# Linear attention and a two-layer feed-forward block in one kernel: a ring of 1280 tokens, accumulators in other banks for late blocks, and plain fp32 projections in the first two batches

## The chip, the cores and the metric

The kernel runs on one core of one Trainium2 chip. The metric is the device time of one execution in microseconds; the kernel before has a median of 1211.63 us over three runs (1211.42 to 1212.69). A profile is one more execution, with its own time. Five engines work side by side, each through its own queue in a fixed order: TensorE (PE in the profile, its weight loads PEld), VectorE (DVE), ScalarE (ACT), GpSimd (POOL) and SyncE (SP), which issues all DMAs here.

## The reference

Eight batches of 576 tokens with 8 heads of 64 features; tokens are then rows of 512 features.

```
def phi(x):
    proj = einsum('bhsd,df->bhsf', x, w_phi)
    proj = proj - max(abs(proj), axis=-1, keepdims=True)
    return concatenate([exp(proj), exp(-proj)], axis=-1)
q_p, k_p = phi(q), phi(k)
kv = einsum('bhsf,bhsd->bhfd', k_p, v)
z = sum(k_p, axis=2)
num = einsum('bhsf,bhfd->bhsd', q_p, kv)
den = einsum('bhsf,bhf->bhs', q_p, z)[..., None] + 1e-06
x = (num / den) with heads joined to rows of 512, 4608 rows
h = x @ w_in                # 512 x 2048
out = maximum(0.01 * h, h) @ w_out      # 2048 x 512
```

The weights w_in and w_out come as 64-bit floats and are taken apart on the chip.

## The kernel before

**Number formats.** Most products are made of three single-pass matmuls in fp32r: an operand is split into a high half (a cast) and a low half (the difference), and high x high, high x low and low x high are added in PSUM. Where both operands of a matmul are plain fp32 tiles, one matmul does it; the trace shows such a matmul as two records.

**Attention.** Two heads form a head pair, number i = 4 b + hp for batch b. `k_phase(i)` loads keys and values, projects 576 tokens in five pieces (`proj`, lines 302 to 306), takes the largest absolute value (VectorE), subtracts it, takes two exponentials (ScalarE) and sums key features times values into kv. `token_q_phase` or `q_phase` does the same for the queries and multiplies by kv; the result is divided by the denominator (line 433 and its like, on GpSimd) and stands in `ring`. Batches 0 and 1 (i under 8) work with plain fp32 kv products, but their projections are three fp32r matmuls per piece: `rk` and `rq` are split before (lines 196, 197, 351, 352, 452, 453, 522 to 524), and the block-diagonal w_phi is held in two halves `bd_h` and `bd_l`. Batch 0 has functions of its own (`first_k_phase`, `first_q_phase`), which borrow the room of weight group 3 (tag "late": `fr1`, `f2`, `f3`, `fr4`) and of the ring. Keys and values 2 and 3 land in the places of 0 and 1 once those are split.

**Weights.** `load_weights` takes 32 pieces of 512 KB: a DMA into one of two stages (one of them in the ring, heads 2 and 3 of batch 1), then three ScalarE and five VectorE instructions that make an fp32 number of the two words of a 64-bit float (lines 159 to 165) and split it into halves (167, 168).

**Feed-forward.** 18 blocks of 256 tokens. `split(i)` (604) splits the block's x from the ring into `xh`, `xl`. `layer1(i, ft)` makes 12 matmuls of 256 columns for each of 16 column groups ft, then a leaky ReLU and a split (625 to 627). `layer2` (630) follows three steps later with 6 matmuls of 512 columns into two PSUM banks of tag "acc", which are emptied to `o` and sent out at the last ft (643 to 646).

**Order.** The loop at 678 interleaves the steps; `advance` draws attention's generators along, up to `room(i)` batches. A scheduler then arranges every engine's instructions by priority (`tc.cur_priority`, lower first): batch 0's keys and first queries, its other queries (`PU`), the rest of attention (`PA`), the weights (`PW`), the feed-forward steps (0). The ring has room for two batches; a batch's places are free once all blocks that read the batch two before are split. PSUM has eight banks: 3 of tag "a", 1 "c", 2 "h", 2 "acc".

Of the kernel before, what the change touches and what calls it, by code (L numbers as in the profile page):

```python
# [44 lines left out]
def attention_moe_kernel(ctx: ExitStack, tc: tile.TileContext, q, k, v, vt, w_phi, w_in, w_out, out):  # L45
# [43 lines left out]
    ring = ct([P, 2, NP, S], F32, "ring")  # L89
# [4 lines left out]
    bd = st([P, 2, 2 * F], F32R, "bd")  # L94
    bd_h, bd_l = bd[:, 0], bd[:, 1]
# [5 lines left out]
    fr1, fr4 = (cp.tile([P, 2048], F32R, tag="late", name=n, bufs=4) for n in ("fr1", "fr4"))  # L101
    f2, f3 = (cp.tile([P, 2048], F32, tag="late", name=n, bufs=4) for n in ("f2", "f3"))
# [8 lines left out]
    def first_load_k(i):  # L111
        if i % 2 == 0:
            rk = st([P, S], F32, "rk")
            rv = st([P, 10, 66], F32, "rv")
        else:
            rk = part(f2, 0, [S])
            rv = part(f2, S, [10, 66])
        nc.sync.dma_start(rk, k[i])
        first_k[i] = rk, rv

    def first_load_v(i):
        rv = first_k[i][1]
# [16 lines left out]
    nc.gpsimd.memset(bd_h.bitcast(F32), 0.0)  # L139
    nc.gpsimd.memset(bd_l.bitcast(F32), 0.0)  # L140
    for j in range(2):
        r = slice(64 * j, 64 * j + 64)
        c = slice(F * j, F * j + F)
        nc.scalar.copy(bd_h[r, c], wr[r])
        nc.vector.tensor_tensor(bd_l[r, c], wr[r], wq_h[r].bitcast(F32), op=ALU.subtract)

    def load_weights():
        n = 0
        stages = [x.rearrange(pat)[:, 0:1024].bitcast(I32) for x, pat in (
            (ring[:, 1, 2:4], "p a s -> p (a s)"), (st([P, 2, 2, U], F32, "qh"), "p a b s -> p (a b s)"))]  # L150
        for ft in range(NFT):
            for which, src in ((0, w_in), (1, w_out)):
                raw = stages[n % 2]
                nc.sync.dma_start(raw, src[:, ft].bitcast(I32))
# [4 lines left out]
                nc.scalar.activation(w, top.bitcast(F32), AF.Abs)
                nc.vector.tensor_scalar(w, w, TINY, HUGE, op0=ALU.max, op1=ALU.min)  # L160
# [4 lines left out]
                nc.vector.tensor_tensor(wi, wi, cr, op=ALU.add)  # L165
# [24 lines left out]
    def k_phase(i):  # L190
        nat = i < NK
        rk, rv = kraw.pop(i)
        ks = st([P, 2, S], F32R, "ks")
        kh, kl = ks[:, 0], ks[:, 1]
        if nat:
            copy_("kh", kh, rk)
            tt_("kl", kl, rk, kh.bitcast(F32), ALU.subtract)
        else:
# [9 lines left out]
        yield  # L208
# [93 lines left out]
    def proj(pk, s, lh, ll, n=P):  # L302
        o = pk[0:n, 256 * s : 256 * s + 256]
        nc.tensor.matmul(o, lhsT=lh, rhs=bd_h, start=True, stop=False)
        nc.tensor.matmul(o, lhsT=lh, rhs=bd_l, start=False, stop=False)
        nc.tensor.matmul(o, lhsT=ll, rhs=bd_h, start=False, stop=True)

    def q_group(qh, ql, t0, w, kvh, x, pm, dn):
# [37 lines left out]
    def token_q_phase(i):  # L346
        b, hp = divmod(i, NP)
        rq = qraw.pop(i)
        qs = st([P, 2, S], F32R, "qs")
        qh, ql = qs[:, 0], qs[:, 1]  # L350
        copy_("qx", qh, rq)
        tt_("qr", ql, rq, qh.bitcast(F32), ALU.subtract)
        if i + 1 < B * NP:
            load_q(i + 1)
        yield
        tq = st([P, 2, 2, U], F32, "tq").rearrange("p a b c -> p a (b c)")
        for g, (t0, w) in enumerate(units):
            yield from q_group(qh, ql, t0, w, kvs_of[i][0], ring[:, b % 2, hp, t0 : t0 + w],
                               tq[:, g % 2, 0:DM].rearrange("p (a f) -> p a f", f=F), st([P, U], F32, "dn")[:, 0:w])

    def q_phase(i):
# [36 lines left out]
        for j in range(2):  # L398
# [16 lines left out]
            for u in range(2):  # L415
# [8 lines left out]
                nc.scalar.copy(ring[rr, b % 2, hp, U * u : U * u + U], nm[0:64])  # L424
# [7 lines left out]
        x = ring[:, b % 2, hp]  # L432
        tt_("x", x, x, dt.rearrange("p a b -> p (a b)"), ALU.mult)
# [9 lines left out]
    def first_k_phase(i):  # L443
        od = i % 2
        rk, rv = first_k.pop(i)
        if od:
            kh = part(fr1, 0, [S])
            kl = part(fr1, S, [S])
        else:
            ks = st([P, 2, S], F32R, "ks")  # L450
            kh, kl = ks[:, 0], ks[:, 1]
        copy_("kh", kh, rk)
        tt_("kl", kl, rk, kh.bitcast(F32), ALU.subtract)
        if i + 2 < NP:
            first_load_k(i + 2)
            if not od:
                first_load_v(i + 2)
        elif i + 2 == NP:
# [49 lines left out]
    def first_load_q(u):  # L508
        t0, w = units[u]
        if u == 0:  # L510
            rq, qh, ql = st([P, NP, w], F32, "qs"), xh, part(fr4, 0, [NP, w])
        elif u == 1:
            rq, qh, ql = part(f3, 1024, [NP, w]), part(fr4, 1024, [NP, w]), part(fr4, 0, [NP, w])
        else:
            rq, qh, ql = st([P, NP, w], F32, "rq"), part(fr1, 1152, [NP, w]), part(fr1, 1408, [NP, w])
        nc.sync.dma_start(rq, q[0:NP, :, t0 : t0 + w].rearrange("a p t -> p a t"))
        first_q[u] = rq, qh, ql

    def first_q_phase(u):
        t0, w = units[u]  # L520
        rq, qh, ql = first_q[u]
        nc.vector.tensor_copy(qh, rq)
        for hp in range(0, NP, 2):
            tt_("ql", ql[:, hp : hp + 2], rq[:, hp : hp + 2], qh[:, hp : hp + 2].bitcast(F32), ALU.subtract)
        yield
        tail = u == 2
        if tail:
            qh, ql = (x.rearrange("p a t -> p (a t)").unsqueeze(1) for x in (qh, ql))
            w = NP * w
        n, ns = P, 2  # L530
        for hp in range(1 if tail else NP):
            pq = pt("a" if u else "acc")
            for s in range(ns):
                proj(pq, s, qh[:, hp, s * P : s * P + n], ql[:, hp, s * P : s * P + n], n)
# [22 lines left out]
            x = ring[:, 0, :, t0:S] if tail else ring[:, 0, hp : hp + 1, t0 : t0 + w]  # L557
# [101 lines left out]
    def room(i):  # L659
        return min(B, 2 + i * T // S) * NP  # L660
# [64 lines left out]
```

## Time and profile before

| | |
|---|---|
| median of three runs | 1211.63 us |
| the profiled execution | 1209.61 us, of which the span is 1207.8 us |
| mean granted TensorE clock | 0.992 |
| busy: PE, PEld | 1160.7 us (96%), 1041.8 us (86%) |
| busy: DVE, ACT, POOL | 785.4 us (65%), 850.7 us (70%), 437.9 us (36%) |
| DMA | 57.01 MB, mean 47 GB/s |

The span runs from the first to the last instruction of the trace. Busy time of PE counts overlapping matmuls once and includes the time in which a matmul drains, so a PE that is fully busy may still start its matmuls further apart than it could. Lines of the profile name a line of the kernel as L619; out<-in are the tiles written and read. Instructions of the helpers `copy_` and `tt_` all stand at L67, L69 or L72 and are told apart by their tiles.

### The profile page before, as it was taken

The numbers are of one execution on the slowest core, as the hardware profiler recorded it, in microseconds if no ns is written. First come the engines' busy times: TensorE is split into PE (matmuls) and PEld (weight loads), VectorE is DVE, ScalarE is ACT, GpSimd is POOL, SyncE is SP. The second block draws the span as 40 slices with busy tenths as digits, with TensorE's granted clock in tenths as the row PEclk, the third lists the DMA queues.
The fourth block names the chain that finished last, engine by engine and source line by source line (L and its number), as shares of the span: only waits on it lengthen the run. The fifth ranks groups of instructions, "written<-read, shape, count | busy, mean of one in ns | idle before, by whom it ended". The sixth has DMA issues, their size and how long they took to land.

```text
span 1207.8 us, 21459 instructions
## 1 busy us (share of the span) xinstructions
PE 1160.7 (96%) x7654; PEld 1041.8 (86%) x7654; DVE 785.4 (65%) x1541; ACT 850.7 (70%) x2144; POOL 437.9 (36%) x436
## 2 busy tenths in 40 slices
PE   6889899999998999999999999999999999999998
PEld 5578688999897988989899999998999998988987
DVE  7999864577787677677787787736777776211111
ACT  6898765778777787878888888846787877433222
POOL 3121121344544454544545454513454544210000
PEclk9999999999998999999999999999999999999999
DMA  6545421011111011111111111100111100000000
GB/s 195 149 126 150 130 80 35 22 49 31 49 32 49 21 27 43 31 49 31 49 32 49 32 40 31 49 22 28 32 49 32 49 1 19 1 18 9 10 18 18
DMA packets 62778, 57.01 MB, mean 47 GB/s; under 512 B 45136, under 2 KB 46288, under 8 KB 62672
## 3 DMA queue, kind: packets, MB, share of 16 engines
q1 hardware_dynamic: 62672, 55.65, 16.4%
q8 instruction: 60, 0.98, 0.4%
q14 instruction: 46, 0.38, 0.1%
HBM read 46.20 MB, written 9.44 MB: 46 GB/s over the span
## 4 chain that ended last, share of the span: by engine, by line
PE 76%; DVE 11%; ACT 7%; issue 3%; DMA 2%; POOL 0%; DVEq 0%; ACTq 0%
PE h L619 10%; PE h L620 10%; PE h L622 10%; PE acc L638 9%; PE acc L640 9%; PE acc L639 9%; PE c L212 6%; PE a L232 2%; PE a L422 2%; PE a L419 2%; PE a L420 2%; PE a L333 1%; DVE ql L165 1%; PE a L379 1%; PE a L380 1%
## 5 line engine op out<-in xcount | busy, mean ns | idle before, releaser
L619 PE MATMUL h<-xh,w0h 128*128 128x256 f32 x1152 | 292.3, 284 | 6.8 <-DVE gl L627 4.5
L620 PE MATMUL h<-xh,w0l 128*128 128x256 f32 x1152 | 289.7, 282 | 0.0
L627 DVE TENSOR_TENSOR gl<-h,gh 128x256 fp32r<-128x256 f32 x288 | 118.5, 416 | 237.4 <-ACT gh L67 210.9
L638 PE MATMUL acc<-w1h,gh 128*128 128x512 f32 x576 | 230.3, 400 | 6.8 <-ACT gh L67 6.1
L619 PEld LDWEIGHTS h<-xh,w0h 128*128 128x128 f32 x1152 | 217.9, 189 | 17.3 <-DVE gl L627 7.7
L639 PE MATMUL acc<-w1l,gh 128*128 128x512 f32 x576 | 228.4, 397 | 0.0
L620 PEld LDWEIGHTS h<-xh,w0l 128*128 128x128 f32 x1152 | 217.8, 189 | 6.0
L625 ACT ACTIVATE h<-h 128x256 f32<-128x256 f32 x288 | 105.3, 368 | 157.2 <-PE h L622 155.3
L640 PE MATMUL acc<-w1h,gl 128*128 128x512 f32 x576 | 204.3, 397 | 0.0
L622 PE MATMUL h<-xl,w0h 128*128 128x256 f32 x1152 | 200.1, 282 | 0.1
L72 POOL TENSOR_TENSOR ql<-eq,qh 128x576 fp32r<-128x576 f32 x96 | 146.1, 1538 | 73.0 <-ACT qh L67 47.8
L622 PEld LDWEIGHTS h<-xl,w0h 128*128 128x128 f32 x1152 | 164.3, 189 | 0.9 <-POOL xl L72 0.3
L72 POOL TENSOR_TENSOR kpl<-ek,kph 128x512 fp32r<-128x512 f32 x72 | 95.4, 1325 | 146.4 <-ACT kph L67 67.5
L638 PEld LDWEIGHTS acc<-w1h,gh 128*128 128x128 f32 x576 | 108.8, 189 | 28.4 <-ACT gh L67 9.8
L639 PEld LDWEIGHTS acc<-w1l,gh 128*128 128x128 f32 x576 | 109.0, 189 | 18.6 <-issue 0.4
L67 ACT CAST gh<-h 128x256 fp32r<-128x256 f32 x288 | 105.2, 373 | 25.6 <-PE acc L639 21.3
L72 POOL TENSOR_TENSOR xl<-ring,xh 128x256 fp32r<-128x256 f32 (+3 forms) x96 | 61.2, 669 | 155.0 <-PE h L622 135.3
L72 POOL TENSOR_TENSOR ring<-ring,mb 128x576 f32<-128x576 f32 (+2 forms) x45 | 49.8, 1108 | 175.0 <-DVE mb L342 45.5
L640 PEld LDWEIGHTS acc<-w1h,gl 128*128 128x128 f32 x576 | 99.5, 189 | 8.5 <-issue 0.4
L202 DVE TENSOR_TENSOR ks<-rk,ks 64x576 fp32r<-64x576 f32 x48 | 53.7, 1118 | 36.5 <-ACT ks L67 35.3
L250 ACT ACTIVATE ek<-pmk 128x256 f32<-128x256 f32 (+1 forms) x128 | 53.4, 417 | 24.3 <-POOL kpl L72 10.3
L212 PE MATMUL c<-kph,vh 128*66 128x256 f32 x240 | 62.3, 282 | 4.0 <-DVE kvl L295 2.2
(225 smaller groups left out, 2366.2 us busy)
## 6 DMA issues: line engine op xcount, KB each, us to landing
out_dram<-o SPq DMA_DIRECT2D x35, 256.0 KB, 2.1
rk<-in_k_dram SPq DMA_DIRECT2D x30, 288.0 KB, 2.8
ring<-in_w_in_dram SPq DMA_DIRECT2D x16, 512.0 KB, 3.6
qh<-in_w_out_dram SPq DMA_DIRECT2D x16, 512.0 KB, 3.7
rq<-in_q_dram SPq DMA_DIRECT2D x28, 288.0 KB, 3.0
rv<-in_v_dram SPq DMA_DIRECT2D x30, 256.0 KB, 3.4
rv<-in_vt_dram SPq DMA_DIRECT2D x60, 32.0 KB, 3.0
f<-in_k_dram SPq DMA_DIRECT2D x2, 288.0 KB, 4.0
```

The lines of the kernel that those rows point to most:

```text
L67: nc.scalar.copy(o, i)
L72: (nc.vector if pick(key) == "v" else nc.gpsimd).tensor_tensor(o, a, b, op=op)
L202: nc.vector.tensor_tensor(ks[n, j], rk[o], ks[o, j].bitcast(F32), op=ALU.subtract)
L212: nc.tensor.matmul(kvp[0 : lt.shape[1], 256 * j : 256 * j + 256], lhsT=lt, rhs=rt, start=first and j == 0, stop=last, skip_group_check=True)
L619: nc.tensor.matmul(ph, lhsT=weight(0, "h", ft)[:, d * P : d * P + P], rhs=xh[:, d], start=d == 0, stop=False)
L620: nc.tensor.matmul(ph, lhsT=weight(0, "l", ft)[:, d * P : d * P + P], rhs=xh[:, d], start=False, stop=False)
L622: nc.tensor.matmul(ph, lhsT=weight(0, "h", ft)[:, d * P : d * P + P], rhs=xl[:, d], start=False, stop=d == NP - 1)
L625: nc.scalar.activation(ph, ph, AF.Prelu, alpha=0.01)
L627: nc.vector.tensor_tensor(gl, ph, gh.bitcast(F32), op=ALU.subtract)
L638: nc.tensor.matmul(a, lhsT=gh[:, ts], rhs=weight(1, "h", ft), start=ft == 0, stop=False)
L639: nc.tensor.matmul(a, lhsT=gh[:, ts], rhs=weight(1, "l", ft), start=False, stop=False)
L640: nc.tensor.matmul(a, lhsT=gl[:, ts], rhs=weight(1, "h", ft), start=False, stop=ft == NFT - 1)
```

## The change

The ring becomes one stretch of 5 blocks (1280 tokens) for each head pair, addressed by token number modulo 1280; a block is never cut, a batch may be cut in two at the end (`places`). `room` counts with the new size. In blocks 15 and 17 the second layer's accumulators are taken from tag "a". `proj` becomes one plain fp32 matmul with a plain `bd`; the splits of keys and queries of batches 0 and 1 go. Keys and values 0 to 3 and the three units of batch 0's queries have landing places of their own, and all keys and values of batch 0 are issued at the start. The weight stages are two pieces of 512 words in two head pairs' places.

```diff
+RW = 5 * T
-    ring = ct([P, 2, NP, S], F32, "ring")
+    ring = ct([P, NP, RW], F32, "ring")
-    bd = st([P, 2, 2 * F], F32R, "bd")
-    bd_h, bd_l = bd[:, 0], bd[:, 1]
+    bd = ct([P, 2 * F], F32, "bd")
...
     def first_load_k(i):
-        if i % 2 == 0:
+        if i == 0:
             rk = st([P, S], F32, "rk")
             rv = st([P, 10, 66], F32, "rv")
         else:
-            rk = part(f2, 0, [S])
-            rv = part(f2, S, [10, 66])
+            x, o = (f2, 0) if i == 1 else (fr1, (i - 2) * S)
+            rk = part(x, o, [S])
+            rv = part(f2 if i % 2 else fr1, 1236 if i == 3 else S * i, [10, 66])
...
     for i in range(2):
         first_load_v(i)
+    for i in range(2, NP):
+        first_load_k(i)
+        first_load_v(i)
...
-        nc.scalar.copy(bd_h[r, c], wr[r])
-        nc.vector.tensor_tensor(bd_l[r, c], wr[r], wq_h[r].bitcast(F32), op=ALU.subtract)
+        nc.scalar.copy(bd[r, c], wr[r])
...
-                nc.sync.dma_start(raw, src[:, ft].bitcast(I32))
-                raw = raw.rearrange("p (n t) -> p n t", t=2)
+                nc.sync.dma_start(raw, src[:, ft].bitcast(I32).rearrange("p (a n) -> p a n", a=2))
+                raw = raw.rearrange("p a (n t) -> p a n t", t=2)
...
-        if nat:
-            copy_("kh", kh, rk)
-            tt_("kl", kl, rk, kh.bitcast(F32), ALU.subtract)
...
-    def proj(pk, s, lh, ll, n=P):
-        o = pk[0:n, 256 * s : 256 * s + 256]
-        nc.tensor.matmul(o, lhsT=lh, rhs=bd_h, start=True, stop=False)
-        nc.tensor.matmul(o, lhsT=lh, rhs=bd_l, start=False, stop=False)
-        nc.tensor.matmul(o, lhsT=ll, rhs=bd_h, start=False, stop=True)
+    def proj(pk, s, x, n=P):
+        nc.tensor.matmul(pk[0:n, 256 * s : 256 * s + 256], lhsT=x, rhs=bd, start=True, stop=True)
...
-    exps = [part(r0, 0, [1024]), part(r0, 1024, [1024]), part(f3, 1024, [1024])]
+    exps = [ring[:, 0, 0:1024], ring[:, 1, 0:1024], part(f3, 1024, [1024])]
...
     def split(i):
+        p = i * T % RW
         for d in range(NP):
-            t0 = 0
-            while t0 < T:
...
+            x = ring[:, d, p : p + T]
+            copy_("xh", xh[:, d], x)
+            tt_("xl", xl[:, d], x, xh[:, d].bitcast(F32), ALU.subtract)
...
-                accs[i, t] = pt("acc")
+                accs[i, t] = pt("a" if i >= NBLK - 3 and i % 2 else "acc")
...
-        return min(B, 2 + i * T // S) * NP
+        return min(B, (RW + i * T) // S) * NP
```

`first_q_phase` and `token_q_phase` lose their casts and subtractions in the same way, and the first `yield` behind them.

More of the change, by code (lines that the diff above doesn't have):

```diff
@@ L99, in attention_moe_kernel @@
     nc.gpsimd.memset(vl[0:64, 8:10].bitcast(F32), 0.0)
-    fr1, fr4 = (cp.tile([P, 2048], F32R, tag="late", name=n, bufs=4) for n in ("fr1", "fr4"))
-    f2, f3 = (cp.tile([P, 2048], F32, tag="late", name=n, bufs=4) for n in ("f2", "f3"))
+    fr1, f2, f3, fr4 = (cp.tile([P, 2048], F32, tag="late", name=n, bufs=4) for n in ("fr1", "f2", "f3", "fr4"))
     def part(x, i, shape):
@@ L143, in attention_moe_kernel @@
         c = slice(F * j, F * j + F)
-        nc.scalar.copy(bd_h[r, c], wr[r])
-        nc.vector.tensor_tensor(bd_l[r, c], wr[r], wq_h[r].bitcast(F32), op=ALU.subtract)
+        nc.scalar.copy(bd[r, c], wr[r])
     def load_weights():
         n = 0
-        stages = [x.rearrange(pat)[:, 0:1024].bitcast(I32) for x, pat in (
-            (ring[:, 1, 2:4], "p a s -> p (a s)"), (st([P, 2, 2, U], F32, "qh"), "p a b s -> p (a b s)"))]
+        stages = [ring[:, 2:4, RW - DM : RW].bitcast(I32),
+                  st([P, 2, 2, U], F32, "qh").rearrange("p a b s -> p a (b s)")[:, :, 0:DM].bitcast(I32)]
         for ft in range(NFT):
@@ L166, in load_weights @@
                 h, l = weight(which, "h", ft), weight(which, "l", ft)
+                w = w.rearrange("p a n -> p (a n)")
                 copy_("h", h, w)
@@ L192, in k_phase @@
         rk, rv = kraw.pop(i)
-        ks = st([P, 2, S], F32R, "ks")
-        kh, kl = ks[:, 0], ks[:, 1]
-        if nat:
-            copy_("kh", kh, rk)
-            tt_("kl", kl, rk, kh.bitcast(F32), ALU.subtract)
-        else:
+        if not nat:
+            ks = st([P, 2, S], F32R, "ks")
             for j in range(2):
@@ L207, in k_phase @@
             load_k(i + 1)
-        yield
+        if not nat:
+            yield
         kvp = pt("c")
@@ L224, in k_phase @@
                     t0 = (2 * g + s) * P if g < 2 else S - P
-                    proj(pk, s, kh[:, t0 : t0 + P], kl[:, t0 : t0 + P])
+                    proj(pk, s, rk[:, t0 : t0 + P])
                 pkv = pk[r, 0 : 256 * w].rearrange("p (a f) -> p a f", f=F)
@@ L313, in q_group @@
             c = slice(t0 + s * P, t0 + s * P + n)
-            proj(pq, s, qh[:, c], ql[:, c], n)
+            proj(pq, s, rq[:, c], n)
         m4 = st([P, 4], F32, "m4")
@@ L348, in token_q_phase, with places @@
         rq = qraw.pop(i)
[L349 to L352, printed above, removed]
         if i + 1 < B * NP:
             load_q(i + 1)
-        yield
         tq = st([P, 2, 2, U], F32, "tq").rearrange("p a b c -> p a (b c)")
         for g, (t0, w) in enumerate(units):
-            yield from q_group(qh, ql, t0, w, kvs_of[i][0], ring[:, b % 2, hp, t0 : t0 + w],
+            yield from q_group(rq, t0, w, kvs_of[i][0], ring[:, hp, b * S + t0 : b * S + t0 + w],
                                tq[:, g % 2, 0:DM].rearrange("p (a f) -> p a f", f=F), st([P, U], F32, "dn")[:, 0:w])
+    def places(b, o, n):
+        p = (b * S + o) % RW
+        c = min(n, RW - p)
+        return [(0, p, c)] + ([(c, 0, n - c)] if c < n else [])
     def q_phase(i):
@@ L423, in q_phase @@
                 rr = slice(64 * j, 64 * j + 64)
-                nc.scalar.copy(ring[rr, b % 2, hp, U * u : U * u + U], nm[0:64])
+                for o, p, c in places(b, U * u, U):
+                    nc.scalar.copy(ring[rr, hp, p : p + c], nm[0:64, o : o + c])
                 nc.scalar.activation(dn[rr, u], nm[64:128], AF.Copy, bias=1e-6)
@@ L431, in q_phase @@
         nc.vector.transpose(blocks(dt), rc.unsqueeze(2).broadcast_to([P, 18, 32]))
-        x = ring[:, b % 2, hp]
-        tt_("x", x, x, dt.rearrange("p a b -> p (a b)"), ALU.mult)
+        dt = dt.rearrange("p a b -> p (a b)")
+        for o, p, c in places(b, 0, S):
+            x = ring[:, hp, p : p + c]
+            tt_("x", x, x, dt[:, o : o + c], ALU.mult)
         yield
@@ L445, in first_k_phase @@
         rk, rv = first_k.pop(i)
[L446 to L458, printed above, removed]
+        if i + 2 == NP:
             load_k(NP)
-        yield
         kvp = pt("h")
@@ L466, in first_k_phase @@
                 t0 = (2 * g + s) * P if g < 2 else S - P
-                proj(pk, s, kh[:, t0 : t0 + P], kl[:, t0 : t0 + P])
+                proj(pk, s, rk[:, t0 : t0 + P])
             r = slice(0, P) if g < 2 else slice(64, P)
@@ L510, in first_load_q @@
         if u == 0:
-            rq, qh, ql = st([P, NP, w], F32, "qs"), xh, part(fr4, 0, [NP, w])
+            rq = st([P, NP, w], F32, "qs")
         elif u == 1:
-            rq, qh, ql = part(f3, 1024, [NP, w]), part(fr4, 1024, [NP, w]), part(fr4, 0, [NP, w])
+            rq = part(fr4, 0, [NP, w])
         else:
-            rq, qh, ql = st([P, NP, w], F32, "rq"), part(fr1, 1152, [NP, w]), part(fr1, 1408, [NP, w])
+            rq = part(fr4, 1024, [NP, w])
         nc.sync.dma_start(rq, q[0:NP, :, t0 : t0 + w].rearrange("a p t -> p a t"))
-        first_q[u] = rq, qh, ql
+        first_q[u] = rq
     def first_q_phase(u):
         t0, w = units[u]
[L521 to L525, printed above, removed]
+        rq = first_q[u]
         tail = u == 2
         if tail:
-            qh, ql = (x.rearrange("p a t -> p (a t)").unsqueeze(1) for x in (qh, ql))
+            rq = rq.rearrange("p a t -> p (a t)").unsqueeze(1)
             w = NP * w
@@ L533, in first_q_phase @@
             for s in range(ns):
-                proj(pq, s, qh[:, hp, s * P : s * P + n], ql[:, hp, s * P : s * P + n], n)
+                proj(pq, s, rq[:, hp, s * P : s * P + n], n)
             m4 = st([P, 4], F32, "m4")
@@ L556, in first_q_phase @@
             dn = st([P, U], F32, "dn")[:, 0:w]
-            x = ring[:, 0, :, t0:S] if tail else ring[:, 0, hp : hp + 1, t0 : t0 + w]
+            x = ring[:, :, t0:S] if tail else ring[:, hp : hp + 1, t0 : t0 + w]
             m = x.shape[1]
```

24 lines of the change are left out of this document (6 added, 18 removed).

## The prediction

> **What bounds the kernel now.** I read the busy time by slices first, then the windows, then the timeline at the places where the windows show a fault. The profiled execution took 1209.61 us, of which 1207.8 are the span; the median of the runs is 1211.63, so 2.0 us are added to what is worked out on the trace.
>
> ```profile
> PE   6889899999998999999999999999999999999998
> DVE  7999864577787677677787787736777776211111
> 0.00:30.00 30.00, 20.40 (x110) 15.92 (x110) 22.58 (x39) 18.29 (x35) 8.97 (x20) 0.95 0.69 196
> 30.00:60.00 30.00, 25.14 (x126) 16.67 (x126) 29.05 (x54) 26.12 (x58) 5.49 (x6) 0.93 0.55 148
> 60.00:90.00 30.00, 24.61 (x153) 21.05 (x154) 29.24 (x63) 28.04 (x65) 8.30 (x9) 1.00 0.41 123
> 90.00:120.00 30.00, 30.00 (x192) 26.20 (x191) 28.54 (x59) 24.54 (x52) 3.83 (x4) 1.00 0.53 148
> 120.00:150.00 30.00, 24.61 (x137) 19.38 (x136) 26.82 (x50) 24.32 (x58) 4.72 (x6) 0.94 0.45 136
> 620.00:680.00 60.00, 60.00 (x417) 55.49 (x416) 47.33 (x91) 51.47 (x130) 31.57 (x28) 1.00 0.15 41
> L165 DVE CUSTOM_DVE_ANT_0 ql<-ql,kvl x32: 641/682/1619, 23.2 to 165.1; 128x1024 uint16<-128x1024 uint16 x32
> ```
>
> A row of the windows gives the stretch and its length, then the busy time of PE, PEld, DVE, ACT and POOL with the number of instructions, the granted clock, the DMA share and GB/s. Two regimes are seen. From about 30 to 120 us VectorE is busy for 28.5 to 29.2 of every 30 us while TensorE has holes: VectorE does batch 0's attention and the 32 steps of the weight decode (L160 to L169), the last of which is at 165.1 us. Layer 1 of block 0 needs all 32, so the end of the decode releases TensorE. From then on TensorE is nearly full (60.00 of 60 in the window from 620), and what counts is its work and its holes.
>
> **The change part by part. (A) The splits of batch 0 and the landing places.** The fp32 data go straight to TensorE, so the casts and subtractions that made high and low halves go. Those on VectorE in the crowded stretch:
>
> ```profile
> L522 DVE CAST xh<-qs x1: 684/684/684, 11.9 to 11.9; 128x1024 fp32r<-128x1024 f32 x1
> L522 DVE CAST fr<-rq x1: 578/578/578, 14.3 to 14.3; 128x256 fp32r<-128x256 f32 x1
> L522 DVE CAST fr<-f x1: 685/685/685, 46.4 to 46.4; 128x1024 fp32r<-128x1024 f32 x1
> 14.81 1.84 DVE L72 TENSOR_TENSOR fr<-f,fr 128x576 fp32r<-128x576 f32 x1
> L72 DVE TENSOR_TENSOR ks<-rk,ks 128x576 fp32r<-128x576 f32 x1 | 0.8, 759 | 0.2 <-ACT ks L67 0.2
> 4.86 0.29 ACT L144 CAST bd<-tq 64x128 fp32r<-64x128 f32 x1
> 6.56 0.42 PE L304 MATMUL acc<-bd,ks 128*128 128x256 f32 x1
> 6.77 0.41 PE L305 MATMUL acc<-bd,ks 128*128 128x256 f32 x1
> 9.36 0.69 DVE L472 TENSOR_REDUCE m<-acc 128x4 f32<-128x512 f32 x1 [1.40 <-PE acc L306]
> ```
>
> That is 0.68 + 0.58 + 0.69 + 1.84 + 0.76 = 4.55 us of VectorE. The first reduction also comes earlier. It waited until 9.36 us for the products with the low half. In the new kernel the last part of bd is there at 4.86 + 0.29 = 5.15 us, and a group of two projections is four records. At the clock of that moment one pass starts 0.21 us after the last (6.56, 6.77), so a record of two passes takes 0.42, and the group ends near 5.2 + 4 x 0.42 + 0.4 = 7.3 us: 2.0 us sooner. The ceiling of (A) is 6.6 us. ScalarE loses the casts of the same tiles (0.67 us each) and so isn't next in line everywhere, but with 28.04 of 30 us busy at 60 to 90 it would take over part of the bound. I take 5.5 of 6.6; the floor is nothing.
>
> Every load of batch 0 is now issued ahead: eight DMAs for keys and values 2 and 3 stand on SP before the queries of unit 0 and the weights. The first decode step comes late, for which VectorE has other work, as the first four key phases are ready at once. I price this at nothing here and put it among the rivals. Weight rows land in two pieces of 2 KB instead of one of 4 KB, and the decode reads two pieces of 256 pairs; no row of the trace has this, the nearest are the present decode steps. I take 0, between -0.1 and +0.1 us for each of 32 steps.
>
> **(B) The projections.** Three single-pass matmuls become one plain fp32 matmul, which the trace shows as two records.
>
> ```profile
> 12.01 1.94 PE L484 MATMUL h<-ring,rv 128*66 128x256 f32 x8 [0.38 <-ACT ring L480]
> 1062.77 0.28 PE L619 MATMUL h<-xh,w0h 128*128 128x256 f32 x1
> 1062.89 0.28 PE L620 MATMUL h<-xh,w0l 128*128 128x256 f32 x1
> L304 PE MATMUL a<-bd,qs 128*128 128x256 f32 x10 | 3.2, 318 | 0.0
> L304 PE MATMUL a<-bd,ks 128*128 128x256 f32 x8 | 2.9, 360 | 0.0
> L304 PE MATMUL a<-bd,qs 128*64 128x256 f32 x3 | 1.4, 468 | 0.0
> ```
>
> Eight plain fp32 records of 256 columns start within 1.94 - 0.38 = 1.56 us: 0.223 us apart. Single-pass ones of the same width start 0.12 apart (1062.77, 1062.89). So a projection costs 2 x 0.223 = 0.45 instead of 3 x 0.12 = 0.36 us, 0.09 more. There are 78 (40 of keys, 38 of queries). The last three rows are from the view of the window 155 to 300: 21 lie where TensorE is full, 21 x 0.09 = 1.9 us. The other 57 (5.1 us) lie where it has holes and cost nothing while the decode is late; if that cover goes, the whole is 7.0. I take +2.
>
> **(C) The late accumulators.** At each of the last three block boundaries TensorE stands still.
>
> ```profile
> 1066.50 0.59 ACT L67 COPY o<-acc 128x512 f32<-128x512 f32 x1 [4.21 <-PE acc L640]
> 1067.09 0.65 ACT L625 ACTIVATE h<-h 128x256 f32<-128x256 f32 x2
> 1067.64 0.66 ACT L67 CAST gh<-h 128x256 fp32r<-128x256 f32 x2
> 1068.08 0.50 PE L638 MATMUL acc<-w1h,gh 128*128 128x512 f32 x1 [0.91 <-ACT gh L67]
> 1114.62 0.50 PE L638 MATMUL acc<-w1h,gh 128*128 128x512 f32 x1 [1.05 <-ACT gh L67]
> 1161.08 0.50 PE L638 MATMUL acc<-w1h,gh 128*128 128x512 f32 x1 [1.05 <-ACT gh L67]
> ```
>
> The copy that empties a bank stands on ScalarE ahead of the leaky ReLU and cast of the next block, and the next block's second layer waits for them, 0.91 + 1.05 + 1.05 = 3.0 us. With banks of tag "a" for blocks 15 and 17 (attention is over) the second layer needs no emptied bank, and the order by priority can put the cast first: -3, or 0 if the copy stays in front.
>
> **(D) Ring and attention's pace.** With 1280 places, batch 2 may start writing after block 1 instead of block 2, batch 6 after block 10 is reached, and a block is one piece, not two. The place where attention holds TensorE up today is block 4:
>
> ```profile
> 376.69 1.56 POOL L72 TENSOR_TENSOR ring<-ring,mb 128x576 f32<-128x576 f32 x1 [2.01 <-DVE mb L431]
> 378.28 0.30 ACT L67 CAST xh<-ring 128x128 fp32r<-128x128 f32 x1 [1.49 <-POOL ring L72]
> 376.00:384.00 8.00, 5.15 (x35) 4.01 (x33) 7.81 (x13) 5.28 (x13) 4.26 (x5) 1.00 0.09 33
> 384.00:388.00 4.00, 1.81 (x8) 1.41 (x9) 3.84 (x10) 2.06 (x5) 1.27 (x1) 0.70 0.63 154
> 388.00:392.00 4.00, 4.00 (x16) 3.65 (x16) 3.86 (x11) 1.91 (x6) 0.00 (x0) 0.50 0.22 72
> ```
>
> Block 4's last piece waits for the last head of batch 2. TensorE is idle for 2.85 + 2.19 = 5.0 us, and then runs at a clock of 0.50 over 4 us, which loses 2.0 more: 7.0 in all. Attention here wasn't waiting for a free place in the ring, so the wider ring alone doesn't cure this. It gains from the shorter heads 4 to 7 (no cast, no subtraction). Bounds: all 7 gone, or a second such stall at another block. I take -2, near the lower loss. [...]
>
> **Sum.** -5.5 + 2 - 3 - 2 = -8.5 us: 1209.61 - 8.5 = 1201.1 for a profiled run, 1203.1 against the median.
>
> **The rivals.** (1) *The startup gain is not passed on.* ScalarE (28.04 of 30) or the weight stages pace the decode, its last step stays near 165 us: (A) is 0, the sum -3, 1208.6 us; with the ReLU copy in front too, 1211.6, no change. For it speaks ScalarE's row; against, VectorE's 29.24.
>
> (2) *Slower: the new loads delay the decode.*
>
> ```profile
> 10.43 0.49 SPq L154 DMA_DIRECT2D ring<-in_w_in_dram  x1
> 16.25 0.67 ACT L159 ACTIVATE ql<-ring 128x512 f32<-128x512 f32 x1
> 18.32 0.59 DVE L160 TENSOR_SCALAR ql<-ql 128x512 f32<-128x512 f32 x1
> rk<-in_k_dram SPq DMA_DIRECT2D x30, 288.0 KB, 2.8
> rv<-in_v_dram SPq DMA_DIRECT2D x30, 256.0 KB, 3.4
> ```
>
> Keys and values 2 and 3 are 2 x (288 + 256 + 64) = 1216 KB, at the 196 GB/s of the first 30 us 6.2 us of transfer ahead of the weights. If VectorE runs dry meanwhile, the decode ends 6.2 us later than in the forecast's starting point instead of 5.5 sooner: -8.5 + 5.5 + 6.2 = +3.2, 1214.8 us. It turns slower once VectorE's added idle time is over 3 us (the remaining gain of B, C and D). Against it: VectorE's first decode step is at 18.32 today, and 12 groups of keys at about 1.2 us keep it busy from 7.3 to 21 us.
>
> (3) *The late accumulators do not do what they say*: the copy stays ahead of the cast on ScalarE, (C) is 0: 1206.1 us.
>
> (4) *Attention comes in time for block 4*: (D) gives all 7 and (A) its 6.6: -6.6 + 2 - 3 - 7 = -14.6, 1197.0 us.
>
> **How the numbers follow.** The forecast gets 0.42, rival 1 0.17 (0.05 of it at 1208.6, the rest at no change), rival 2 0.16, rival 3 0.10, rival 4 0.15. A measurement here tells about 0.2% (2.4 us) from no change. Faster: 0.42 + 0.05 + 0.10 + 0.15 = 0.72; same 0.12; slower 0.16. The likeliest time is 1203. The range reaches 3 us beyond rival 4 for the unknown price of the decode's pieces (3.2 us either way), takes in rivals 1 and 3, and ends at 1213, before rival 2; what it leaves out is that rival and the far tails, about 0.2.
>
> **What would show it.** (A) right: the last L165 ends near 158 us, VectorE stays over 28 of 30 us, the first reduction starts near 7.3. Wrong: it stays at 165, or VectorE idles between 10 and 30 us. (B): the proj line's records start 0.22 us apart, and after 155 us some 21 pairs remain. (C): no idle time over 0.3 us before the first L638 of blocks 15, 16 and 17. (D): no window under 0.9 clock between 200 and 1000 us. The forecast is wrong above all if attention, whose instruction order is arranged anew, starves TensorE at another block: one stall like that at 376 us is worth 7 us, as much as (A).

## The result and the profile after

Before 1211.53 us (1210.53 to 1212.69), after **1225.02 us** (1222.17 to 1227.36): medians of four runs each, a ratio of 1.011, 95% interval 1.0087 to 1.0133, so 13.5 us slower. The profiled execution took 1227.36 us, its span is 1225.6. The forecast was 1203, with a range that ended at 1213. In the rows of after the decode keeps L159 to L165, layer 1 is L592 to L595, layer 2 L611 to L613, and `copy_` and `tt_` stand at L68 and L73.

The slices of after, rows as in the prediction, and GB/s:

```profile
PE   8878877999999999999999999999999999999998
DVE  4458888576877787877777878787777852111111
GB/s 187 1 45 150 135 156 153 33 45 48 31 40 29 40 30 47 32 49 30 49 31 49 31 40 39 27 43 32 48 31 48 1 18 9 10 18 10 9 18 18
```

TensorE has holes through seven slices (214 us) where before it had them through five. The second slice moves 1 GB/s: no weights arrive in it. The windows of after:

```profile
0.00:30.00 30.00, 24.45 (x101) 17.44 (x102) 14.29 (x25) 13.25 (x28) 1.45 (x14) 1.00 0.68 191
30.00:60.00 30.00, 26.86 (x137) 19.07 (x135) 15.12 (x29) 18.68 (x46) 4.36 (x6) 1.00 0.00 1
60.00:90.00 30.00, 23.23 (x102) 18.12 (x103) 16.49 (x37) 17.63 (x42) 4.35 (x6) 0.83 0.16 45
320.00:440.00 120.00, 120.00 (x830) 110.69 (x829) 94.23 (x183) 98.69 (x254) 62.47 (x57) 1.00 0.14 40
440.00:620.00 180.00, 179.37 (x1238) 165.19 (x1237) 142.25 (x261) 148.78 (x376) 89.87 (x83) 1.00 0.13 37
1040.00:1190.00 150.00, 146.84 (x935) 132.59 (x934) 24.41 (x56) 42.18 (x117) 8.47 (x12) 1.00 0.04 14
```

From 30 to 90 us VectorE is busy for some 16 of every 30 us, where it had over 29 before. It isn't short of time, it is short of work: the decode is missing. Two steps of the decode by source line, first and last start:

```profile
L159 ACT ACTIVATE ql<-ring x16: 649/676/701, 81.2 to 206.7; 128x512 f32<-128x512 f32 x16
L165 DVE CUSTOM_DVE_ANT_0 ql<-ql,kvl x32: 651/684/947, 83.8 to 213.9; 128x1024 uint16<-128x1024 uint16 x32
```

The decode begins at 81.2 us (16.25 before) and its last step starts at 213.9 (165.1 before), with each step as long as it was (median of L159 676 ns, 670 before; of L165 684, 682 before). The timeline of after at its begin:

```profile
79.89 0.72 POOL L73 TENSOR_TENSOR ring<-ring,mb 128x256 f32<-128x256 f32 x1 [3.96 <-DVE mb L555]
80.95 0.38 ACT L549 ACTIVATE dn<-c 64x256 f32<-64x256 f32 x1
81.24 0.65 ACT L159 ACTIVATE ql<-ring 128x512 f32<-128x512 f32 x1
82.90 0.69 DVE L162 SCALAR_TENSOR_TENSOR ql<-ring,ql 128x512 int32<-128x512 int32 x1
83.67 0.37 SPq L154 DMA_DIRECT2D ring<-in_w_in_dram  x1
```

The first decode step follows a multiplication of x by GpSimd (the fourth head pair of batch 0's second unit of queries; its last unit comes later, at 90.2 us), and the next load of weights follows the decode step that frees its stage. The listing of the built program (number of the instruction on ScalarE, line, tiles, what it waits for) names it:

```
before:  15 L159 ACTIVATE ql<-ring 128x512 [waits DMAHW7_49]
after:  103 L159 ACTIVATE ql<-ring 128x512 [waits DMAHW7_49,Pool_49]
```

Before, the step waits for its load alone. After, it waits for GpSimd as well, and so is put 88 places later. Its stage, `ring[:, 2:4, RW-DM:RW]`, is two pieces, tokens 768 to 1279 of head pairs 2 and 3. They share no place with batch 0 (tokens 0 to 575), but the places of batch 0 in pair 3 lie between them. The theory is that a strided read over both pieces is recorded as covering what lies between.

The delay isn't passed on whole: 49 us at block 1, 18 at the end. For the windows of before that answer to the fourth and fifth row:

```profile
320.00:440.00 120.00, 113.28 (x756) 103.28 (x757) 87.13 (x166) 93.28 (x238) 55.55 (x51) 0.97 0.14 36
440.00:620.00 180.00, 174.76 (x1196) 159.56 (x1195) 138.09 (x268) 141.88 (x362) 88.61 (x82) 1.00 0.14 39
```

Before, TensorE idles for 6.7 and 5.2 us there; after, for 0 and 0.6. While the feed-forward waited for weights, attention ran on.

### The profile page after: what moved, and what is told of

Read it like the earlier page. It is cut to its first block, busy times and chain, and to the rows that moved or that the text cites. A ratio compares the mean times of both kernels' runs of the same rounds, so it can differ in the third digit from the quotient of the medians.

```text
span 1225.6 us, 21299 instructions
## 1 busy us (share of the span) xinstructions
PE 1177.0 (96%) x7576; PEld 1046.8 (85%) x7576; DVE 796.8 (65%) x1532; ACT 851.1 (69%) x2132; POOL 417.2 (34%) x410
## 4 chain that ended last, share of the span: by engine, by line
PE 81%; ACT 7%; DVE 5%; DMA 3%; issue 2%; POOL 0%; SPq 0%; DVEq 0%; ACTq 0%
PE h L593 10%; PE h L592 10%; PE h L595 10%; PE acc L611 9%; PE acc L613 8%; PE acc L612 8%; PE c L210 6%; PE a L230 2%; PE a L301 2%; PE a L415 2%; PE a L414 2%; DMA qh<-in_w_out_dram 2%; PE a L417 2%; PE h L469 1%; PE a L611 1%
## 5 line engine op out<-in xcount | busy, mean ns | idle before, releaser
L592 PE MATMUL h<-xh,w0h 128*128 128x256 f32 x1152 | 294.3, 284 | 2.8 <-ACT w0h L68 2.8
L592 PEld LDWEIGHTS h<-xh,w0h 128*128 128x128 f32 x1152 | 219.0, 190 | 13.2 <-ACT w0h L68 4.3
L611 PE MATMUL acc<-w1h,gh 128*128 128x512 f32 x512 | 205.2, 403 | 15.9 <-ACT gh L68 13.2
L598 ACT ACTIVATE h<-h 128x256 f32<-128x256 f32 x288 | 104.8, 368 | 165.1 <-PE h L595 160.2
L612 PE MATMUL acc<-w1l,gh 128*128 128x512 f32 x512 | 202.1, 396 | 0.0
L595 PE MATMUL h<-xl,w0h 128*128 128x256 f32 x1152 | 199.0, 282 | 0.0
L613 PE MATMUL acc<-w1h,gl 128*128 128x512 f32 x512 | 181.5, 397 | 0.5 <-DVE gl L600 0.5
L595 PEld LDWEIGHTS h<-xl,w0h 128*128 128x128 f32 x1152 | 164.7, 190 | 0.9
L73 POOL TENSOR_TENSOR ql<-eq,qh 128x576 fp32r<-128x576 f32 x96 | 147.7, 1555 | 41.0 <-ACT qh L68 37.0
L73 POOL TENSOR_TENSOR kpl<-ek,kph 128x512 fp32r<-128x512 f32 x72 | 97.1, 1349 | 142.1 <-PE c L210 66.4
L68 ACT CAST gh<-h 128x256 fp32r<-128x256 f32 x288 | 104.5, 372 | 50.4 <-PE acc L612 43.1
L611 PEld LDWEIGHTS acc<-w1h,gh 128*128 128x128 f32 x512 | 96.3, 189 | 35.4 <-ACT gh L68 18.4
L73 POOL TENSOR_TENSOR ring<-ring,mb 128x256 f32<-128x256 f32 (+7 forms) x57 | 56.3, 997 | 188.1 <-DVE mb L555 55.9
L612 PEld LDWEIGHTS acc<-w1l,gh 128*128 128x128 f32 x512 | 96.6, 189 | 15.9 <-DVE w1l L73 0.3
L73 POOL TENSOR_TENSOR xl<-ring,xh 128x256 fp32r<-128x256 f32 x72 | 51.4, 744 | 170.8 <-PE h L595 144.1
L613 PEld LDWEIGHTS acc<-w1h,gl 128*128 128x128 f32 x512 | 89.3, 190 | 9.4 <-DVE gl L600 1.3
L199 DVE TENSOR_TENSOR ks<-rk,ks 64x576 fp32r<-64x576 f32 x48 | 73.6, 1533 | 35.0 <-ACT ks L68 33.6
L73 POOL TENSOR_TENSOR vl<-rv,vh 128x512 fp32r<-128x512 f32 (+1 forms) x48 | 46.7, 973 | 72.8 <-ACT vh L68 70.9
```

The costliest lines, as they stand in the source:

```text
L68: nc.scalar.copy(o, i)
L73: (nc.vector if pick(key) == "v" else nc.gpsimd).tensor_tensor(o, a, b, op=op)
L592: nc.tensor.matmul(ph, lhsT=weight(0, "h", ft)[:, d * P : d * P + P], rhs=xh[:, d], start=d == 0, stop=False)
L595: nc.tensor.matmul(ph, lhsT=weight(0, "h", ft)[:, d * P : d * P + P], rhs=xl[:, d], start=False, stop=d == NP - 1)
L598: nc.scalar.activation(ph, ph, AF.Prelu, alpha=0.01)
L611: nc.tensor.matmul(a, lhsT=gh[:, ts], rhs=weight(1, "h", ft), start=ft == 0, stop=False)
```

## The experiments

If that is so, the recorded wait makes the loss. The rivals: the late loads of weights (rival 2 of the prediction), the strided reads in themselves, and the wider ring's order of work. A stall that leaves one place can come back at another (e7 has 4.5 us of it), so the starts of several blocks are compared and not the total alone; their table stands behind the last run.

**e1: the whole change, first stage in a tile of its own.**

```diff
-        stages = [ring[:, 2:4, RW - DM : RW].bitcast(I32),
+        stages = [st([P, 2, S], F32, "ks")[:, :, 0:DM].bitcast(I32),
```

> The changed kernel with the first weight stage moved out of the ring into the idle tile of tag ks. Theory (the first decode step waits for the last write of batch 0's x, because the strided read of the stage in the ring is taken to cover the places between its two pieces): first decode step before 30 us instead of 81, last one before 172 instead of 214, and 1183 to 1203 us. Rival 1 (plain fp32 projections make TensorE the bound of the start): decode begins early but ends after 195, 1212 us or more. Rival 2 (SyncE is held by the load of keys 5, which waits for projections): the third weight load stays after 65 us, 1208 us or more.

1206.48 us, ratio 0.9957 (0.9942 to 0.9972). The last decode step by source line:

```profile
L165 DVE CUSTOM_DVE_ANT_0 ql<-ql,kvl x32: 642/682/1210, 27.8 to 166.3; 128x1024 uint16<-128x1024 uint16 x32
```

With the wait gone the kernel is 1225.0 - 1206.5 = 18.5 us faster; the two-piece reads are still in it. The time is 3.5 us above the upper end of what was expected.

**e2: the ring alone, on the kernel before.**

```diff
+RW = 5 * T
-    ring = ct([P, 2, NP, S], F32, "ring")
+    ring = ct([P, NP, RW], F32, "ring")
...
+        stages = [ring[:, 2:4, RW - DM : RW].bitcast(I32),
...
-        return min(B, 2 + i * T // S) * NP
+        return min(B, (RW + i * T) // S) * NP
```

> The kernel before with the ring of 1280 tokens alone (its stage, exps, places, split and room), with split fp32r projections, old landing places and old accumulators. Theory: first decode step after 70 us and 1218 to 1235 us, the loss being in the ring part alone. Rivals 1 and 2 (the loss comes with the projections or the key loads): first decode step near 17 us, 1203 to 1213 us.

1234.43 us, ratio 1.0192 (1.0168 to 1.0216), with the first decode step at 79.1 us: the loss lies in this part.

**e3: the projections and landing places alone, on the old ring.**

```diff
+    bd = ct([P, 2 * F], F32, "bd")
...
+    for i in range(2, NP):
+        first_load_k(i)
+        first_load_v(i)
...
+        nc.tensor.matmul(pk[0:n, 256 * s : 256 * s + 256], lhsT=x, rhs=bd, start=True, stop=True)
```

> The kernel before with the plain fp32 projections and the landing places alone, on the old ring and with old accumulators. Theory: decode begins before 35 us and 1196 to 1210 us, a gain of 2 to 15 as parts A and B of the prediction have it. Rival 1 (TensorE-bound start): 1215 us or more. Rival 2 (SyncE held): 1212 us or more, and a wait of over 20 us on SyncE for the key load.

1200.32 us, ratio 0.9911 (0.9895 to 0.9928): 10.5 us faster. Its decode begins at 22.9 us (16.2 before) and ends as before.

**e4: the late accumulators alone.**

```diff
-                accs[i, t] = pt("acc")
+                accs[i, t] = pt("a" if i >= NBLK - 3 and i % 2 else "acc")
```

> The kernel before with the late accumulators in attention's banks alone. Theory (the copy that empties the old banks stays ahead of the next cast in ScalarE's order): TensorE is idle for about 1.0 us before the first second-layer matmul of blocks 15, 16 and 17 as before, and the time within 1.5 us of the kernel before. Rival (the banks do free it): those waits are gone and the time is 2.5 to 3.5 us less.

One run: 1211.02 beside 1210.83 us, no gain. TensorE waits 0.91, 1.05 and 1.05 us before the second layer of blocks 15, 16 and 17, the same as before.

**e5 and e6: the stage read by head pair**, in the whole change (e5) and in the ring alone (e6).

```diff
-                nc.scalar.activation(w, top.bitcast(F32), AF.Abs)
+                for a in range(2):
+                    nc.scalar.activation(w[:, a], top[:, a].bitcast(F32), AF.Abs)
```

The two other reads of the stage are cut in the same way.

> The changed kernel with its stage left in the ring, but each of the three instructions that read a stage made two, one for each head pair's piece. Theory (only the shape of the read, which spans both pieces, makes the false wait): first decode step before 30 us, last one before 175, 1202 to 1214 us, a little over the run with the stage in ks for the 3 x 32 additional instructions. Rival (the place in the ring itself holds it): first step stays after 70 us, 1220 us or more.

> The kernel before with the ring of 1280 tokens alone, its stage read by head. Theory (without the false wait the ring costs some 6 us still, as stage in ks against projections alone has it, since batches 2, 4 and 6 are cut in two): 1214 to 1222 us. Rival (those 6 us are chance of the new order, the ring is neutral): 1205 to 1213 us.

e5: 1213.0 us, ratio 1.0011 (1.0002 to 1.0021); e6: 1211.46, ratio 0.9997 (0.9973 to 1.0021), with ten runs from 1204.9 to 1216.3. So e6 missed the theory's 1214 to 1222: beside the kernel before, the ring without the wait shows no cost, though its runs spread widely. The first decode step of e5 by source line:

```profile
L160 ACT ACTIVATE ql<-ring x32: 416/436/473, 22.4 to 161.2; 128x256 f32<-128x256 f32 x32
```

The stage stayed where it was and only the reads were cut, and the wait is gone: it is the span of the read that makes it, not the place. e5 stays 6.5 us above e1. Three steps cut in two are 3 x 32 more instructions, but these are over soon after 170 us (its last L168, the L165 of after, starts at 169.6), and at block 7 e5 is still ahead (573.3 us, e1 575.3); at block 17 it is behind (1158.9, e1 1152.6). Why it loses time there isn't shown.

**e7: e3 with the decode held back by an added tile**, until batch 0's last x is done. L164, which is L165 of after, first starts at 87.2 us (83.8 in after) and last at 208.6 (213.9).

```diff
+    hold = st([P, DM], I32, "kvl")
+    nc.gpsimd.tensor_copy(hold[:, 0:1].bitcast(F32), ring[:, 0, 3, S - 1 : S])
     load_weights()
```

> Projections alone (old ring) with the decode held back by hand: an additional tile of tag kvl, into which GpSimd copies one element of batch 0's last x, stands ahead of the first decode step's tile. Theory (the late decode costs some 25 us in the start and, as attention runs ahead meanwhile, takes the stall before block 4 away): 1214 to 1230 us, last decode step after 195 us, TensorE idle under 4 us in the windows from 300 to 600. Rival (the wider ring took the stall away): the idle time at block 4 stays over 3 us there.

1235.16 us, ratio 1.0216 (1.0184 to 1.0248): a late decode on the old ring costs 34.8 us over e3, more than expected and more than the 18.5 us of e1, though its last step comes sooner than in after. At block 7 e7 and after stand level (598.6 us in both); at block 17 e7 is 6.9 us later. Why isn't shown. Its windows, and those of e3 (with two more, used further on):

```profile
320.00:440.00 120.00, 119.19 (x821) 109.50 (x820) 90.90 (x176) 95.69 (x245) 59.72 (x57) 1.00 0.14 38
440.00:620.00 180.00, 175.55 (x1192) 159.42 (x1190) 133.48 (x254) 143.88 (x364) 88.09 (x82) 1.00 0.13 37
```

```profile
320.00:440.00 120.00, 114.90 (x772) 105.28 (x772) 89.17 (x168) 96.97 (x247) 59.29 (x55) 0.97 0.13 34
360.00:392.00 32.00, 26.90 (x163) 23.76 (x163) 23.64 (x44) 24.61 (x66) 17.49 (x20) 0.89 0.17 46
440.00:620.00 180.00, 179.21 (x1236) 164.71 (x1235) 134.72 (x266) 148.12 (x373) 91.40 (x85) 1.00 0.14 39
1040.00:1190.00 150.00, 146.99 (x933) 132.24 (x932) 23.89 (x55) 43.34 (x123) 9.05 (x16) 1.00 0.03 12
```

The hole of 5.1 us from 320 to 440 shrinks to 0.8 on the old ring too, so the late decode removes it and not the wider ring; 4.5 us of holes come from 440 to 620.

**e8 and e9: the late block boundaries**, both on e3. e8 has the accumulators in "a" and all late copies on VectorE, e9 gives layer 1 idle "a" banks instead.

```diff
-                copy_("o", o, accs[i, t])
+                (nc.vector.tensor_copy if i >= NBLK - 5 else nc.scalar.copy if t == 0 else nc.vector.tensor_copy)(o, accs[i, t])
```

```diff
-        ph = pt("h")[:, 0:T]
+        ph = pt("a" if i >= NBLK - 3 and ft % 2 else "h")[:, 0:T]
```

> Projections alone, with late accumulators in attention's banks and all copies out of the accumulators from block 13 on put on VectorE. Theory (the copy on ScalarE ahead of the cast is what held TensorE at the late boundaries): no idle time over 0.4 us before the first second-layer matmul of blocks 15, 16 and 17, and 2.5 to 4.5 us less than projections alone, 1196 to 1198 us. Rival (something else holds it there): the waits of about 1 us stay, 1199 to 1202 us.

> Projections alone with the idle banks of attention given to the first layer instead: in blocks 15 to 17 every second group of columns puts its 256 sums into a bank of tag a. Theory (after e8: TensorE stands at the late boundaries because both first-layer banks wait for ReLU and cast, not because of the accumulators): idle time before the first second-layer matmul of blocks 15 to 17 under 0.4 us each, 2 to 4 us less than projections alone, 1196.5 to 1198.5 us. Rival (the order keeps another wait there): 1199.5 to 1202 us.

e8 1200.71 us, nothing over e3; **e9 1196.87** (1196.72 to 1197.05), ratio 0.9881 (0.9863 to 0.9899), the best of all. The start of block 15's second layer in the timeline of after, and that of block 16 in e8:

```profile
1084.54 0.59 ACT L68 COPY o<-acc 128x512 f32<-128x512 f32 x1 [4.78 <-PE acc L613]
1085.03 0.65 ACT L598 ACTIVATE h<-h 128x256 f32<-128x256 f32 x2
1085.59 0.66 ACT L68 CAST gh<-h 128x256 fp32r<-128x256 f32 x2
1086.03 0.50 PE L611 MATMUL a<-w1h,gh 128*128 128x512 f32 x1 [1.05 <-ACT gh L68]
```

```profile
1105.30 0.69 DVE L613 COPY o<-a 128x512 f32<-128x512 f32 x1 [4.33 <-PE a L609]
1105.41 0.65 ACT L594 ACTIVATE h<-h 128x256 f32<-128x256 f32 x2 [4.90 <-PE h L591]
1105.96 0.66 ACT L67 CAST gh<-h 128x256 fp32r<-128x256 f32 x2
1106.40 0.50 PE L607 MATMUL acc<-w1h,gh 128*128 128x512 f32 x1 [0.68 <-ACT gh L67]
```

In after the copy stands ahead of the ReLU though the new block writes "a" banks. In e8 it is on another engine, and TensorE still waits 0.68 us (0.91 at block 15, 0.68 at block 17; e3 has 0.91, 1.05 and 1.05): for the ReLU and the cast of two layer-1 banks that were filled together ("x2"). With more of those banks TensorE has layer-1 work of its own to go on with. In e9 the waits at all three blocks are gone. Its window, beside 146.99 in e3:

```profile
1040.00:1190.00 150.00, 150.00 (x955) 135.67 (x955) 24.58 (x56) 44.48 (x125) 9.05 (x16) 1.00 0.03 12
```

**e10 and e11: the first two weight loads ahead of keys and values 2 and 3**, on e3 and on e9.

```diff
+    nc.sync.dma_start(stages[0], w_in[:, 0].bitcast(I32))
+    nc.sync.dma_start(stages[1], w_out[:, 0].bitcast(I32))
     for i in range(2, NP):
         first_load_k(i)
         first_load_v(i)
```

> Projections alone, with the first two weight loads issued ahead of the loads of keys and values 2 and 3. Theory (the VectorE time saved by part A was lost because the decode began some 6 us later behind those loads): first decode step before 18 us, last one 3 to 7 us before 164.7, and 1194 to 1198 us. Rival (something else paces the decode, so its end does not follow its start): last step within 2 us of 164.7, 1199 to 1203 us.

> Projections alone with both of these. Theory: the gains of the two add up, as one lies before 170 us and the other after 1050. If only one of them gains, this has that one's time within 1.5 us.

1200.97 us (ratio 0.9915, 0.9897 to 0.9933) and 1197.62: no gain. Yet the mechanism took place. By source line, timeline and windows of e10:

```profile
L167 DVE CUSTOM_DVE_ANT_0 ql<-ql,kvl x32: 642/682/779, 17.9 to 155.0; 128x1024 uint16<-128x1024 uint16 x32
```

```profile
375.79 1.56 POOL L72 TENSOR_TENSOR ring<-ring,mb 128x576 f32<-128x576 f32 x1 [1.70 <-DVE mb L422]
```

```profile
360.00:392.00 32.00, 24.70 (x140) 22.01 (x139) 24.37 (x44) 23.59 (x60) 17.05 (x20) 0.84 0.17 46
372.00:376.00 4.00, 1.50 (x8) 0.86 (x6) 3.81 (x8) 2.16 (x6) 0.83 (x2) 0.94 0.18 68
376.00:380.00 4.00, 3.42 (x15) 3.42 (x16) 3.91 (x9) 1.64 (x3) 1.88 (x2) 0.50 0.00 0
```

The decode's last step comes 9.7 us sooner than in e3 (164.7), block 1 starts at 157.0 instead of 166.6. But the multiplication that finishes batch 2's x starts at 375.8, 2.2 later than in e3 (373.6), and from 360 to 392 TensorE idles 7.3 us instead of 5.1, at a clock of 0.84 instead of 0.89. Block 5 starts at 443.9, in e3 at 442.6. What the decode gains is gone at block 5; between them lies block 4, whose x comes late.

**e12: two-piece stages on the old ring, with nothing of batch 0 between the pieces.**

```diff
+        stages = [ring[:, 1, 2:4, S - DM : S].bitcast(I32),
```

> Projections alone with the weight stages in two pieces of 512 words as in the changed kernel, but both pieces of the first stage in batch 1's part of the old ring, so that nothing of batch 0 lies between them. Theory (the pieces cost nothing, only what lies between them does): first decode step before 30 us and 1198.5 to 1202.5 us. Rival (the shorter rows and the strided reads cost, which would explain 6 us between the stage in ks and projections alone): 1204 to 1209 us.

1200.31 us, ratio 0.9906 (0.9885 to 0.9928), that of e3 (1200.32): pieces as such cost nothing here. Its first decode step waits for its load alone in the listing, as e1's and e5's do.

**e13 to e15: why e1 is still 6.2 us above e3.** e13 is e1 with `room` as before; e14 is e3 with x cut where the new ring would cut it; e15 is e3 with the stage of e1.

```diff
-        return min(B, (RW + i * T) // S) * NP
+        return min(B, 2 + i * T // S) * NP
```

```diff
+    def places(b, o, n):
+        p = (b * S + o) % 1280
+        c = min(n, 1280 - p)
+        return [(0, c)] + ([(c, n - c)] if c < n else [])
...
+                for o, c in places(b, U * u, U):
+                    nc.scalar.copy(ring[rr, b % 2, hp, U * u + o : U * u + o + c], nm[0:64, o : o + c])
...
+        for o, c in places(b, 0, S):
+            x = ring[:, b % 2, hp, o : o + c]
+            tt_("x", x, x, dt[:, o : o + c], ALU.mult)
```

```diff
+            (st([P, 2, S], F32, "ks"), "p a s -> p (a s)"), (st([P, 2, 2, U], F32, "qh"), "p a b s -> p (a b s)"))]
```

> The kernel of e1 (the whole change with the first weight stage in a tile of tag ks) with the old rule for how far attention may run ahead: a batch is let in after the same block as before, though the ring has room for more. e1 took 1206.5 and the old ring with the projections (e3) 1200.3; 6.2 us are open. Theory: the wider ring's earlier admission puts attention's instructions in a worse order and holds blocks 4 to 10 up; then this run is near e3, 1200 to 1203, block 4 to block 8 no longer than in e3 (267 us). Rival: the cuts at the ring's end or the stage's place cost it; then it stays at 1205 to 1208.

> e3 (old ring, projections and landing places) with the copies of x and the multiplications of batches 2, 4 and 6 cut in two where the wider ring would cut them, at token 128, 256 and 384 of the batch: seven to twelve more multiplications on GpSimd and a dozen more copies on ScalarE, nothing else moved. Theory that the earlier admission is the cause: no change against e3, 1199.5 to 1201.5. Rival, that the cuts cost the 6.2 us: 1204 to 1207, and the last x of batch 2 comes 1 us or more later than in e3 (373.55).

> e3 with the first weight stage in a tile of tag ks, as in e1, instead of the ring's places. While the decode lasts, the keys have one buffer less. Theory that the earlier admission is the cause: no change against e3, 1199.5 to 1201.5. Rival, that the buffer taken from the keys costs attention the time: 1204 to 1207, and head 7's last x later than in e3 (243.26).

e13 1205.91 (ratio 0.9956, 0.9943 to 0.9969), e14 **1205.39** (0.9949, 0.9933 to 0.9964), e15 1200.02 (0.9902, 0.9888 to 0.9916). The theory that the earlier admission is the cause falls; the rival stands: in this kernel the cuts cost 5.1 of the 6.2 us, the stage's place nothing, and 1.1 is within the spread. TensorE's busy time in e14 from 440 to 620 us, where e3 has 179.21:

```profile
440.00:620.00 180.00, 175.54 (x1204) 160.77 (x1203) 137.57 (x267) 143.70 (x371) 91.81 (x87) 1.00 0.14 39
```

Starts read from the timelines (us): the last decode step (L165 in before), the first layer-1 matmul of some blocks, and GpSimd's multiplication that finishes x of the last head pair of batch 2 (needed by block 4) and batch 3 (needed by block 6).

| | last decode step | block 1 | x of batch 2 | block 5 | x of batch 3 | block 7 | block 17 |
|---|---|---|---|---|---|---|---|
| before | 165.1 | 166.9 | 376.7 | 445.2 | 511.5 | 576.9 | 1155.6 |
| e3 | 164.7 | 166.6 | 373.6 | 442.6 | 502.5 | 570.8 | 1146.2 |
| e10 | 155.0 | 157.0 | 375.8 | 443.9 | 503.8 | 572.1 | 1147.4 |
| e14 | 166.3 | 168.3 | 374.9 | 443.0 | 509.2 | 575.8 | 1152.1 |
| e1 | 166.3 | 168.1 | 374.9 | 445.5 | 507.2 | 575.3 | 1152.6 |
| after | 213.9 | 216.0 | 387.4 | 470.8 | 515.3 | 598.6 | 1173.4 |

In the first five rows the order of block 7 is that of batch 3's x and not that of block 1: the faster kernels are those whose attention is early. After is the exception: there the feed-forward is the later of the two (block 4 starts at 407.5, 20 us behind batch 2's x).

## Why the prediction was wrong

**The step that failed** is in (A): "Weight rows land in two pieces ... I take 0, between -0.1 and +0.1 us for each of 32 steps." The length of a step was right (L165 takes 684 ns in the median, 682 before). What had to be asked was which earlier writes a read of that shape would be made to wait for. The move turned one contiguous stage into a read that spans batch 0's places, and put the whole decode behind most of batch 0's attention, to 81.2 us: a term of 18.5 us (after against e1) where the sum had 0. The size depends on the kernel around it: the same wait, taken out by reading piece by piece, is worth 12.0 us in the whole change (e5) and 23.0 in the ring alone (e2 against e6).

**Rival 2** had the direction and the symptom, VectorE short of work while the decode is late, but not the cause: its price was 6.2 us of transfer. That delay does exist: the decode of e3 begins 6.7 us later than before, and e10, which takes it away, ends the decode 9.7 us sooner than e3. But e10 takes as long as e3, so here it costs nothing.

**(A), -5.5:** the saving was there, its way to the end was not. The first reduction starts at 7.4 us in e3 (7.6 in after), near the 7.3 that was asked for: the pace of 0.42 us a record was taken from the rows at 6.56 and 6.77 us, and the first eight records of after start 0.44 apart (L301, 5.55 to 9.10 us). That this pace is the clock's isn't shown, since the trace lists 1.00 from 6 to 10 us in both kernels. And from its first step to its last the decode takes 148.9 us before, 141.8 in e3 and 143.4 in e10: 7.1 and 5.5 less. In e3 the late loads use this up, so that the decode ends as before; that is what rival 1 foresaw, but not for its reason. And "the end of the decode releases TensorE" holds as far as block 1: e10's decode ends 9.7 us sooner than e3's, and both take the same time. e3's gain goes with attention instead: batch 2's x comes 3.1 us sooner than before and batch 3's 9.0, and block 17 starts 9.4 us sooner. That the casts removed are what made x early is likely, but no run separates them. That e3 lay in its expected range was in part luck: the range was made from (A) and (B), with (A)'s gain coming through the decode.

**(B), +2:** its records start 0.22 us apart as expected (L301 of after at 14.40 us: four in 1.03 us, each 0.38 long); what they cost isn't told apart from the gain in e3, where A, B and D, without the ring's part of D, were put at -5.5 together and measured -10.5.

**(C), -3:** nothing (e4), the result of rival 3. But its reason, the copy ahead of the cast, isn't the whole one either: e8 moves the copy away, and 0.91, 0.68 and 0.68 us of waits stay. The size of 3.0 us was right and the remedy wrong: with more layer-1 banks the waits go (e9, 3.45 us less than e3).

**(D), -2:** the sign asked for was no window under 0.9 of the clock from 200 to 1000 us. After has 0.52 from 202 to 209 us, ahead of block 1, and 1.00 from there to 1000. The wider ring isn't the reason: e7, on the old ring, has 1.00 from 320 to 620 us too, where before and e3 have 0.97 from 320 to 440. Attention's pace, taken as -2, goes with most of e3's gain (block 7 with batch 3's x, in the table). And the ring has a price that the text didn't name: x of batches 2, 4 and 6 written in two parts, 5.1 us in e14. It isn't a price of the cuts everywhere: e6 has them too and is no slower than the kernel before.

So the parts are: e3 -10.5, the cuts +5.1, the recorded wait +18.5, the late accumulators 0: +13.1, beside +13.5 measured. These are steps of one chain of kernels, so that they add up is no test of its own; another order of steps gives other sizes, as e5 and e6 show. How the cuts make batch 3's x 6.7 us late stays open: their instructions' own time is small (the copies of x take 19.5 us from 240 to 640 in e14, 18.7 in e3), so the order of the work may have a part in it, but no run separates that.

## What to carry to other kernels

When a buffer moves, ask of every read of it what lies between its first and last byte: the waits may be set by that span, and the listing of waits shows it before any run. Where two streams of work feed one engine, look for the place at which each must have arrived; a gain in the stream that is early there can be given back, as the 9.7 us of e10's decode were. At a block boundary try idle PSUM banks for the layer whose output the next instruction waits for; here they were worth 3.45 us in the first layer and nothing in the second.

## What the hardware showed that was not expected

The clock fell with no single wait over 1.42 us in the 10 us before. In e10 it was 0.50 from 376 to 380 us, right behind the stretch in which TensorE was busy for 1.50 of 4 us; the timeline of e10 gives TensorE's waits:

```profile
369.07 0.54 PE L413 MATMUL a<-ql,kvh 128*128 128x288 f32 x2 [1.42 <-POOL ql L72]
371.25 0.45 PE L211 MATMUL c<-kpl,vh 128*66 128x256 f32 x2 [0.64 <-DVE kpl L72]
372.94 0.40 PE L370 MATMUL a<-qs,wq 128*128 128x288 f32 x1 [0.74 <-DVE pmk L236]
375.01 0.40 PE L370 MATMUL a<-qs,wq 128*128 128x288 f32 x1 [1.31 <-DVE tq L372]
376.58 0.61 PE L370 MATMUL a<-qs,wq 128*128 128x288 f32 x1 [1.04 <-DVE pmk L236]
```

From 366 to 377 us there are these five waits, of 0.64 to 1.42 us and 5.15 us together. Whether these brought the clock down, and by what, isn't shown. And one program can vary by itself: ten runs of e6 lay between 1204.9 and 1216.3 us, where four of e9 kept within 0.4. The cause of that isn't known.
